# Another order of the parts of a pair of heads, and another start of the GLU, in an attention + soft-MoE + GLU kernel

## Chip, cores and metric

One Trainium2 chip, of which one core is used. The metric is the device time of one execution in microseconds; three executions of the kernel before took 492.02, 494.66 and 494.78 us, median 494.66 us.

## The reference

```python
# q, k, v: (4 batches, 8 heads, 576 tokens, 64)
q_rot, k_rot = rotate(q), rotate(k)                 # rope
attn = softmax(scale * q_rot @ k_rot.T) @ v         # -> x, 2304 tokens x 512
# soft MoE: 8 experts with 4 slots each, 512 -> 1024 -> 512
logits = x @ phi
d = softmax over the tokens (axis 0) of logits
slot_out[e] = maximum((d.T @ x)[e] @ w1[e], 0) @ w2[e]
y = (softmax over the slots of logits) @ slot_out
# "GLU": 512 -> 768 -> 512
h = maximum(maximum(y @ g1, y @ g2), y @ g3)
out = h @ w_out
```

## The kernel before, in words

All matmuls take float32 data; where full precision is wanted, a number is split into a high part (a cast to fp32r, on ACT) and a low part (the rest, on DVE or POOL), and the products of the parts are added up in PSUM.

**Attention.** The work goes by pairs of heads, 16 pairs `g`, each with nine units `n = 9*g + i`: a unit is 128 columns of scores (S, L342/L354 on PE), their maximum (L359 on DVE), the exponential (L371 on ACT), its transposition (T, L380/L382/L386 on PE) and the copy out of PSUM (Te, L403/L405 on ACT, L408/L411 on DVE). Then come the product with v (PV, L430/L433 on PE) into `u`, whose high part ACT takes (L442) and whose low part DVE takes (L440), a matmul that gives the tokens' x and their logits (L471), and sums for the softmax over all tokens of a batch.

The pair's inputs are made while the pair before it runs: POOL applies rope to q, k and the 64 rest tokens' rows r (L220 to L223), PE transposes them (L272 for q and k, L255 for r, tiles `tq<g>q`, `tq<g>k`, `tq<g>r`), ACT takes the high part (L283/L285), DVE the low part (L294/L297) into `qkt`, and SP's DMA queue stacks these into `qst` and `kst` (L303, eight transfers a pair), which the scores read.

**Weights.** Between these, 32 blocks of weights that come in an eight byte form are converted to float32 (tiles `raw`, `cv`, `cx`: ACT L596/L620, DVE L610, L613, L615, L618, POOL L622/L624, loads L582, stores L590 to `wod` and `wmd`). Two small DVE steps (L950, tile `xr`) make the low part of phi. SP also queues the loads of the expert weights (`wt`, L150), of q and k (L196), of their rest rows (`rr`, L186/L187) and of v (L202/L209). Each `wt` load takes the place of one whose last reader is done.

**What sets the order.** The program runs under a manual schedule: each part of each pair is put into one list with a time in units, `at_(9*g + value, part)`, the list is sorted, and that is the program order of every engine. The values are the table `TIMES`: for pairs 2 to 14 the same ones each, `first` for the opening (pairs 0 and 1), `last` for pair 15, `fill...` for the conversion, `loadw` for the weight loads. An engine takes its instructions in that order and waits on semaphores for what they need.

**Tail.** After the attention the slots' inputs go through the experts (h L742, its transposition L732, `ops` L758), limited by the weights' transfers; at the end of this stream SP queues the GLU's weights (L766/L768 `wm`, L771 `wof`). The MoE output is then multiplied with the GLU's first weights per slot (tiles `tq`, three PSUM banks, L801), so that a piece of 128 hidden columns costs one matmul of 128 rows for each of the three weights. `stacked(f)` splits such a piece: a cast on ACT (L814) and a subtraction on DVE (L815), into the tile of f: `ts8`, `ts9`, `ts23`, `tsxr`, `tslg`, `tssit` for f = 0 to 5; f and f+3 share a bank of `tq`. `prepare(f)` splits w_out's rows of piece f: a cast on ACT (L709), a subtraction on POOL (L710). `emit_h(k, f)` is three matmuls (L837, `g`), the maximum of three on DVE (L846; a copy on ACT and two DVE maxima, L842 to L844, for a few), then a split: cast on ACT (L856), subtraction on POOL (L857). Three matmuls for each 128 tokens and piece add to the output (L892, `r`). k = 0 is the 256 rest tokens, k = 1 to 4 are 512 tokens of a batch each. The `g` tiles are in two pools of three PSUM banks with one tile each; the first has banks that are free early, the second those of `tq`:

```python
i = run["h"] = run.get("h", -1) + 1
ps = ps_g[(i - 1) % 2 if i else 0].tile([128, 3, 512], F32, tag="g", name=f"g{k}_{f}")
```

## Time and profile before

| what | value |
|---|---|
| median of three executions | 494.66 us (492.02 to 494.78) |
| the profiled execution | 491.53 us |
| its span, first to last instruction | 489.70 us |
| outside the span | 1.83 us |
| PE busy | 466.1 us (95%) |
| DVE, ACT, POOL busy | 347.9, 293.7, 279.3 us |
| bytes moved | 105.67 MB, mean 216 GB/s |
| mean granted TensorE clock | 0.997 |

All rows below and all durations are of the one profiled execution; "idle before" is the time for which an engine stood before an instruction, and the arrow names what ended it. PE is the engine that is busy nearly always, with three stretches where it is not: the opening, the end of the weights' stream and the start of the GLU.

### The profile page before, as it was taken

The numbers are of one execution on the slowest core, as the hardware profiler recorded it, in microseconds if no ns is written. First come the engines' busy times: TensorE is split into PE (matmuls) and PEld (weight loads), VectorE is DVE, ScalarE is ACT, GpSimd is POOL, SyncE is SP. The second block draws the span as 40 slices with busy tenths as digits, with TensorE's granted clock in tenths as the row PEclk, the third lists the DMA queues.
The fourth block names the chain that finished last, engine by engine and source line by source line (L and its number), as shares of the span: only waits on it lengthen the run. The fifth ranks groups of instructions, "written<-read, shape, count | busy, mean of one in ns | idle before, by whom it ended". The sixth has DMA issues, their size and how long they took to land. (4 is left out here: it accounts for less than half of the span.)

```text
span 489.7 us, 9779 instructions
## 1 busy us (share of the span) xinstructions
PE 466.1 (95%) x3392; PEld 348.9 (71%) x3392; DVE 347.9 (71%) x663; ACT 293.7 (60%) x652; POOL 279.3 (57%) x374
## 2 busy tenths in 40 slices
PE   8789899999999999999999999998998799999996
PEld 7678677787786877868768777774334567888885
DVE  7869899987889889899989898566221367544520
ACT  2677688786887877788878778651201344322311
POOL 5989678878697796769986743011000276423420
PEclk9999999999999999999999999999999899999999
DMA  8589999998899899998987837999999401111111
GB/s 212 148 232 249 291 254 267 272 272 230 246 248 296 222 286 272 228 263 219 232 197 179 210 100 183 306 363 391 388 386 407 189 0 44 65 44 65 43 66 64
DMA packets 73121, 105.67 MB, mean 216 GB/s; under 512 B 12144, under 2 KB 41456, under 8 KB 72560
## 3 DMA queue, kind: packets, MB, share of 16 engines
q1 hardware_dynamic: 73072, 105.04, 74.5%
q8 instruction: 27, 0.44, 0.4%
q14 instruction: 22, 0.18, 0.1%
HBM read 66.98 MB, written 11.01 MB: 159 GB/s over the span
## 5 line engine op out<-in xcount | busy, mean ns | idle before, releaser
L359 DVE TENSOR_REDUCE nm<-s 128x1 f32<-128x576 f32 x144 | 107.7, 749 | 20.4 <-PE s L354 17.0
L371 ACT ACTIVATE P<-s,nm 128x576 f32<-128x576 f32 x144 | 106.9, 744 | 23.2 <-DVE nm L359 22.0
L354 PE MATMUL s<-kst,qst 128*128 128x288 f32 x600 | 108.2, 311 | 4.2 <-DMA kst<-qkt 1.5
L380 PE MATMUL s<-ident,P 128*128 128x128 f32 x576 | 90.9, 281 | 2.5 <-ACT P L371 2.3
L354 PEld LDWEIGHTS s<-kst,qst 128*128 128x128 f32 x600 | 85.0, 190 | 9.1 <-PE s L354 2.6
L380 PEld LDWEIGHTS s<-ident,P 128*128 128x128 f32 x576 | 63.9, 140 | 26.3 <-ACT P L371 14.3
L892 PE MATMUL r<-wo,h 128*128 128x512 f32 x324 | 79.7, 396 | 0.6 <-ACT h L856 0.2
L430 PE MATMUL u<-pt,vn 128*64 128x256 f32 (+1 forms) x512 | 72.2, 414 | 0.0
L892 PEld LDWEIGHTS r<-wo,h 128*128 128x128 f32 x324 | 61.2, 190 | 15.2 <-POOL h L857 0.9
L857 POOL TENSOR_TENSOR h<-hf,h 128x512 fp32r<-128x512 f32 (+1 forms) x30 | 35.4, 1181 | 45.3 <-ACT h L856 45.2
L846 DVE TENSOR_REDUCE hf<-g 128x512 f32<-128x1536 f32 (+1 forms) x26 | 40.8, 1599 | 28.1 <-PE g L837 23.9
L403 ACT COPY pt<-s 128x512 f32<-128x512 f32 x64 | 37.5, 585 | 22.6 <-PE s L380 21.3
L405 ACT COPY pt<-s 128x640 f32<-128x640 f32 x64 | 44.5, 695 | 7.8 <-PE s L382 7.5
L430 PEld LDWEIGHTS u<-pt,vn 128*64 128x64 f32 x512 | 32.5, 136 | 22.1 <-issue 5.1
L856 ACT CAST h<-hf 128x512 fp32r<-128x512 f32 (+1 forms) x30 | 17.3, 578 | 50.7 <-DVE hf L846 45.3
L622 POOL TENSOR_TENSOR raw<-raw 128x384 f32<-128x384 f32 x32 | 26.5, 828 | 36.3 <-ACT raw L620 30.2
L624 POOL TENSOR_TENSOR cv<-cv,raw 128x384 f32<-128x384 f32 x32 | 33.0, 1030 | 2.5
L710 POOL TENSOR_TENSOR wo<-wof,wo 128x512 fp32r<-128x512 f32 x6 | 7.6, 1280 | 44.5 <-ACT wo L709 44.5
L615 DVE SCALAR_TENSOR_TENSOR cv<-raw,cv 128x384 uint32<-128x384 uint32 x32 | 29.2, 912 | 0.4
L371 ACT ACTIVATION_READ_ACCUMULATOR P<-s,nm 128x1 f32 x144 | 28.7, 199 | 0.0
L471 PE MATMUL x<-xr,ut 128*128 128x256 f32 x160 | 26.4, 294 | 0.0
L471 PEld LDWEIGHTS x<-xr,ut 128*128 128x128 f32 x160 | 21.4, 189 | 1.0 <-DVE ut L440 0.2
(363 smaller groups left out, 761.6 us busy)
## 6 DMA issues: line engine op xcount, KB each, us to landing
wt<-in_moe_w_dram SPq DMA_DIRECT2D x32, 1024.0 KB, 10.0
qst<-qkt SPq DMA_DIRECT2D x60, 288.0 KB, 6.3
raw<-in_moe_w_dram SPq DMA_DIRECT2D x24, 384.0 KB, 5.3
kst<-qkt SPq DMA_DIRECT2D x30, 160.0 KB, 5.2
wmd<-cv SPq DMA_DIRECT2D x24, 192.0 KB, 4.1
kst<-qkt SPq DMA_DIRECT2D x30, 144.0 KB, 5.0
vn<-in_v_dram SPq DMA_DIRECT2D x16, 256.0 KB, 6.7
wm<-wmd SPq DMA_DIRECT2D x4, 1024.0 KB, 14.5
```

The lines of the kernel that those rows point to most:

```text
L354: nc.tensor.matmul(s[:, h, 0:288], l, r[:, 288 * h:288 * h + 288], start=(i == 0), stop=(i == len(todo) - 1))
L359: nc.vector.tensor_reduce(out=nm[n], in_=st[n][:, :, 0:288], axis=AX.XY, op=ALU.max, negate=True)
L371: nc.scalar.activation(out=dst.rearrange("p (h c) -> p h c", h=2), in_=s[:, :, 0:288], func=AF.Exp, bias=nm.pop(n), accum_out=acc)
L380: nc.tensor.transpose(s[:, 0, 128 * c:128 * c + 128], p[:, c0 + 128 * c:c0 + 128 * c + 128], ident)
L403: copy(out=o[:, 0:4, w + q0:w + q0 + 128], in_=src[:, 0:4, :])
L405: copy(out=o[:, 0:5, q0:q0 + 128], in_=src[:, 0:5, :])
L430: nc.tensor.matmul(u[r, 0:q1 - q0], vn[g][:, x, 64 * c:64 * c + 64], o[:, c, c0 + q0:c0 + q1], start=(c == 0), stop=False)
L471: nc.tensor.matmul(ps[:, 256 * i:256 * i + 256], utf[:, S * z + 128 * t:S * z + 128 * t + 128], xr[:, 0:hp + 2:hp + 1, :], start=(z == 0), ...
L624: nc.gpsimd.tensor_tensor(out=t3, in0=t3, in1=hf, op=ALU.add)
L846: nc.vector.tensor_reduce(out=h, in_=ps[:, :, 0:n].rearrange("p m n -> p n m"), axis=AX.X, op=ALU.max)
L857: nc.gpsimd.tensor_tensor(out=lo, in0=h, in1=hi.bitcast(F32), op=ALU.subtract)
L892: nc.tensor.matmul(p, a[:, s_], w, start=(f == 0 and z == 0), stop=(f == NF - 1 and z == 2))
```

## The change

All values of `TIMES` but a few are other numbers, so that the program order of the engines is another one; and the start of the GLU is written in another order. The code, and two lines of the table:

```diff
- 'loadw': -3.321369,
+ 'loadw': 15.022565,
- 'stackk': -4.533007,
+ 'stackk': -6.992883,
...
-        for f in range(2):
-            prepare(f)
+
+        FO = [0, 1, 3, 4, 2, 5]
+        prepare(0)
...
-            if f == 0:
+            if k not in hid:
...
-            ps = ps_g[(i - 1) % 2 if i else 0].tile([128, 3, 512], F32, tag="g", name=f"g{k}_{f}")
+            ps = ps_g[(i - 1) % 2 if i > 2 else 0].tile([128, 3, 512], F32, tag="g", name=f"g{k}_{f}")
...
-        for f in (0, 1, 3, 4):
+        for f in (0, 1, 3):
             stacked(f)
-        emit_h(0, 0)
+        prepare(1)
+        emit_h(0, 0, (0,))
+        stacked(4)
+        emit_h(0, 0, (1,))
+        emit_h(0, 1, (0,))
         stacked(2)
+        emit_h(0, 1, (1,))
         stacked(5)
-        emit_h(0, 1)
...
-                for f in range(NF):
+                for z0, f in enumerate(range(NF) if k else FO):
                     while rows and rows[0][0] <= step:
-                        emit_h(*divmod(rows.pop(0)[1], NF))
-                    if k == 0 and f + 2 < NF:
-                        prepare(f + 2)
+                        k_, f_ = divmod(rows.pop(0)[1], NF)
+                        emit_h(k_, f_ if k_ else FO[f_])
+                    if k == 0 and z0 + 2 < NF:
+                        prepare(FO[z0 + 2])
...
-                            nc.tensor.matmul(p, a[:, s_], w, start=(f == 0 and z == 0), stop=(f == NF - 1 and z == 2))
+                            nc.tensor.matmul(p, a[:, s_], w, start=(z0 == 0 and z == 0), stop=(z0 == NF - 1 and z == 2))
```

`emit_h(k, f, (0,))` is the matmuls and the maximum alone, `(1,)` the split alone. The piece order of k = 0 is now 0, 1, 3, 4, 2, 5, and of the `g` tiles the first four (i = 0 to 3) are in the first pool and i = 4 is the first in the second pool, where before i = 2 was.

Set side by side, the two program orders differ in four stretches.

**The opening, pairs 0 to 2.** DVE before, from the second maximum of pair 0 (`nm1`) to the fifth (`nm4`); `cx0`, `cv0` and `raw0` are the conversion of the first block, `xr` is phi's low part:

```order
L359 TENSOR_REDUCE nm1_274<-s1_266 128x1
L610 TENSOR_SCALAR cx0_286<-cv0_284 128x3x128
L613 TENSOR_SCALAR cv0_284<-cx0_286 128x384
L294 SCALAR_TENSOR_TENSOR qkt_109<-tq1q_297,qkt_109 128x512
L359 TENSOR_REDUCE nm2_312<-s2_290 128x1
L950 TENSOR_TENSOR xr_65<-early_106,xr_65 64x4x32
L297 TENSOR_TENSOR qkt_109<-tq1r_323,qkt_109 128x2x2x64
L615 SCALAR_TENSOR_TENSOR cv0_284<-raw0_276,cv0_284 128x384
L359 TENSOR_REDUCE nm3_342<-s3_328 128x1
L950 TENSOR_TENSOR xr_65<-early_106,xr_65 64x4x32
L297 TENSOR_TENSOR qkt_109<-tq1k_351,qkt_109 128x512
L618 TENSOR_SCALAR raw0_276<-cv0_284 128x3x128
L359 TENSOR_REDUCE nm4_393<-s4_366 128x1
```

DVE now, the same stretch (L956 is L950 of before):

```order
L359 TENSOR_REDUCE nm1_274<-s1_266 128x1
L294 SCALAR_TENSOR_TENSOR qkt_109<-tq1q_292,qkt_109 128x512
L359 TENSOR_REDUCE nm2_300<-s2_285 128x1
L297 TENSOR_TENSOR qkt_109<-tq1r_317,qkt_109 128x2x2x64
L359 TENSOR_REDUCE nm3_331<-s3_323 128x1
L956 TENSOR_TENSOR xr_65<-early_106,xr_65 64x4x32
L610 TENSOR_SCALAR cx0_343<-cv0_341 128x3x128
L613 TENSOR_SCALAR cv0_341<-cx0_343 128x384
L615 SCALAR_TENSOR_TENSOR cv0_341<-raw0_276,cv0_341 128x384
L956 TENSOR_TENSOR xr_65<-early_106,xr_65 64x4x32
L618 TENSOR_SCALAR raw0_276<-cv0_341 128x3x128
L359 TENSOR_REDUCE nm4_384<-s4_333 128x1
```

The six instructions that stood one by one between the maxima now stand in a row between the fourth and the fifth. On ACT the first block's cast (L596) that stood between the first two exponentials comes after the third.

SP's queue before, from the stacking of pair 2's q on:

```order
L303 DMA qst0_101<-qkt_109 64x2x576 x4
L186 DMA rr1_649<-in_q_dram 64x8x64
L187 DMA rr1_649<-in_k_dram 64x8x64
L590 DMA wod_71<-cv2_503 128x384
L582 DMA raw5_681<-in_moe2_w_out_dram 128x256
L582 DMA raw5_681<-in_moe2_w_out_dram 128x2x256
L303 DMA kst0_103<-qkt_109 64x576 x2
L303 DMA kst0_103<-qkt_109 64x640 x2
L196 DMA qn4_716<-in_q_dram 128x2x256
L196 DMA kn4_718<-in_k_dram 128x2x256
L150 DMA wt1_730<-in_moe_w1_dram 128x4x512
```

and now:

```order
L303 DMA qst0_101<-qkt_109 64x2x576 x4
L303 DMA kst0_103<-qkt_109 64x576 x2
L303 DMA kst0_103<-qkt_109 64x640 x2
L590 DMA wod_71<-cv2_500 128x384
L582 DMA raw5_675<-in_moe2_w_out_dram 128x256
L582 DMA raw5_675<-in_moe2_w_out_dram 128x2x256
L196 DMA qn4_679<-in_q_dram 128x2x256
L196 DMA kn4_681<-in_k_dram 128x2x256
L186 DMA rr1_688<-in_q_dram 64x8x64
L187 DMA rr1_688<-in_k_dram 64x8x64
```

The four transfers of `kst` for pair 2 come right behind those of `qst`, ahead of two loads of rest rows, a store and two or three loads; the first `wt` load of this place is gone: the first ten such loads stand two pairs later than before, and so does the rest of the row until the end of the attention, where the last 22 stand as before.

**Pairs 2 to 15.** One thing moves: the rest rows' transposition, cast and subtraction (`tq<g>r`) go from behind the last products of the pair before to right behind the first scores of the new pair, and POOL's rope takes r after k. ACT before, at the start of pair 8 (`s72` is its first unit, `s70` and `u7` belong to pair 7):

```order
L620 ACTIVATE raw17_2115<-raw17_2115 128x3x128
L596 ACTIVATE cv18_2393<-raw18_2220 128x384
L405 COPY pt1_7_2322<-s70_2346 128x5x128
L371 ACTIVATE P0_110,sums8_2420<-s72_2406,nm72_2412 128x576
L442 CAST ut_112<-u7_0_2382 128x256
L285 CAST qkt_109<-tq9r_2430 128x2x2x64
L403 COPY pt0_8_2450<-s72_2406 128x4x128
L371 ACTIVATE P0_110,sums8_2420<-s73_2434,nm73_2448 128x576
```

and now:

```order
L596 ACTIVATE cv18_2397<-raw18_2216 128x384
L405 COPY pt1_7_2322<-s70_2346 128x5x128
L285 CAST qkt_109<-tq9r_2412 128x2x2x64
L371 ACTIVATE P0_110,sums8_2426<-s72_2407,nm72_2421 128x576
L442 CAST ut_112<-u7_0_2372 128x256
L403 COPY pt0_8_2450<-s72_2407 128x4x128
L371 ACTIVATE P0_110,sums8_2426<-s73_2431,nm73_2448 128x576
```

The cast of `tq9r` (L285) stands ahead of the first exponential of the pair, no longer behind `ut`. On DVE the subtraction of r (L297) stands likewise ahead of that of `ut` (L440).

**Pair 15** has its last sums and x parts in a slightly other order; SP's last stores and loads and the 22 `wt` loads are as before.

**The GLU's start.** ACT before (`h40_0` and `h6_0` are the high parts of k = 0, `hf0_f` the maxima of its piece f, `wo422` and `wo6` those of w_out):

```order
L709 CAST wo422_5016<-wof0_4883 128x512 x2
L814 CAST ts8_5023<-tq0_4924 64x384
L814 CAST ts9_5024<-tq1_4925 64x384
L814 CAST tsxr_5026<-tq0_4924 64x384
L814 CAST tslg_5027<-tq1_4925 64x384
L856 CAST h40_0_5050<-hf0_0_5057 128x256
L814 CAST ts23_5025<-tq2_4926 64x384
L814 CAST tssit_5028<-tq2_4926 64x384
L856 CAST h40_0_5050<-hf0_1_5069 128x256
L709 CAST wo422_5016<-wof0_4883 128x512
L856 CAST h40_0_5050<-hf0_2_5087 128x256
L709 CAST wo422_5016<-wof0_4883 128x512
```

and now (L815 and L857 are L814 and L856 of before):

```order
L709 CAST wo422_5016<-wof0_4883 128x512
L815 CAST ts8_5021<-tq0_4924 64x384
L815 CAST ts9_5022<-tq1_4925 64x384
L815 CAST tsxr_5024<-tq0_4924 64x384
L709 CAST wo422_5016<-wof0_4883 128x512
L815 CAST tslg_5025<-tq1_4925 64x384
L857 CAST h40_0_5048<-hf0_0_5055 128x256
L815 CAST ts23_5023<-tq2_4926 64x384
L857 CAST h40_0_5048<-hf0_1_5065 128x256
L815 CAST tssit_5026<-tq2_4926 64x384
L709 CAST wo422_5016<-wof0_4883 128x512
L857 CAST h40_0_5048<-hf0_3_5087 128x256
```

One cast of w_out stands ahead of the first piece's cast instead of two, the second after three pieces. DVE before:

```order
L815 TENSOR_TENSOR ts8_5023<-tq0_4924,ts8_5023 64x384
L815 TENSOR_TENSOR ts9_5024<-tq1_4925,ts9_5024 64x384
L815 TENSOR_TENSOR tsxr_5026<-tq0_4924,tsxr_5026 64x384
L815 TENSOR_TENSOR tslg_5027<-tq1_4925,tslg_5027 64x384
L846 TENSOR_REDUCE hf0_0_5057<-g0_0_5053 128x256
L815 TENSOR_TENSOR ts23_5025<-tq2_4926,ts23_5025 64x384
L815 TENSOR_TENSOR tssit_5028<-tq2_4926,tssit_5028 64x384
L846 TENSOR_REDUCE hf0_1_5069<-g0_1_5065 128x256
L846 TENSOR_REDUCE hf0_2_5087<-g0_2_5083 128x256
L846 TENSOR_REDUCE hf0_3_5103<-g0_3_5099 128x256
L846 TENSOR_REDUCE hf0_4_5111<-g0_4_5107 128x256
```

and now (L816 and L847 are L815 and L846 of before):

```order
L816 TENSOR_TENSOR ts8_5021<-tq0_4924,ts8_5021 64x384
L816 TENSOR_TENSOR ts9_5022<-tq1_4925,ts9_5022 64x384
L816 TENSOR_TENSOR tsxr_5024<-tq0_4924,tsxr_5024 64x384
L847 TENSOR_REDUCE hf0_0_5055<-g0_0_5051 128x256
L816 TENSOR_TENSOR tslg_5025<-tq1_4925,tslg_5025 64x384
L847 TENSOR_REDUCE hf0_1_5065<-g0_1_5061 128x256
L816 TENSOR_TENSOR ts23_5023<-tq2_4926,ts23_5023 64x384
L816 TENSOR_TENSOR tssit_5026<-tq2_4926,tssit_5026 64x384
L847 TENSOR_REDUCE hf0_3_5087<-g0_3_5083 128x256
L847 TENSOR_REDUCE hf0_4_5103<-g0_4_5099 128x256
L847 TENSOR_REDUCE hf0_2_5111<-g0_2_5107 128x256
```

The first maximum stands behind three subtractions (before: four), the second behind four (before: six), and the piece of `tsxr` is the third to be reduced, that of `ts23` the fifth.

## Rows read from the trace of the kernel before

**Rows 1.** Busy time of each engine by stretch, with granted clock, DMA share, GB/s.
```profile
core 0: us, PE busy (x) PEld busy (x) DVE busy (x) ACT busy (x) POOL busy (x), PEclk, DMA share, GB/s
...
56.00:306.00 250.00, 246.76 (x1956) 190.75 (x1954) 223.84 (x463) 200.44 (x458) 188.25 (x259) 1.00 0.90 236
...
340.00:386.00 46.00, 43.04 (x396) 18.21 (x396) 10.11 (x22) 9.13 (x16) 1.53 (x3) 1.00 1.03 387
...
414.00:489.70 75.70, 71.84 (x316) 58.93 (x314) 28.00 (x20) 20.21 (x35) 22.56 (x18) 1.00 0.15 56
```
**Rows 2.** Timeline, end of the weights' stream: start, us, engine line op, [idle before <-releaser].
```profile
371.72 1.06 PE L758 MATMUL ops<-wt,hts 128*32 128x512 f32 x8 [1.66 <-DMA wt<-in_moe_w_dram]
383.85 1.25 ACT L709 CAST wo<-wof 128x512 fp32r<-128x512 f32 x2 [2.48 <-DMA wof<-wod]
```
**Rows 3.** Timeline, the opening (pair 0), on DVE and PE.
```profile
15.68 0.55 DVE L610 TENSOR_SCALAR cx<-cv 128x384 f32<-128x384 f32 x1 [0.68 <-ACT cv L596]
...
18.27 0.98 DVE L950 TENSOR_TENSOR xr<-early,xr 64x128 fp32r<-64x128 f32 x1
...
19.62 1.23 DVE L615 SCALAR_TENSOR_TENSOR cv<-raw,cv 128x384 uint32<-128x384 uint32 x1
...
20.78 0.74 DVE L359 TENSOR_REDUCE nm<-s 128x1 f32<-128x576 f32 x1
...
23.97 1.41 DVE L359 TENSOR_REDUCE nm<-s 128x1 f32<-128x576 f32 x2
...
36.81 0.76 PE L354 MATMUL s<-kst,qst 128*128 128x288 f32 x4 [0.38 <-DVE pt L411]
```
**Rows 4.** One line, L615, all its 32 instructions: min/median/max in ns.
```profile
L615 DVE SCALAR_TENSOR_TENSOR cv<-raw,cv x32: 539/770/1678, 19.6 to 296.4; 128x384 uint32<-128x384 uint32 x32
```
**Rows 5.** Timeline, stacking of pair 2: SP's queue, DVE's low part, PE's first scores.
```profile
46.81 3.45 SPq L303 DMA_DIRECT2D kst<-qkt  x4
...
42.70 0.68 DVE L297 TENSOR_TENSOR qkt<-tq2k,qkt 128x512 fp32r<-128x512 f32 x1
...
54.30 0.77 PE L354 MATMUL s<-kst,qst 128*128 128x288 f32 x4 [1.47 <-DMA kst<-qkt]
```
**Rows 6.** Timeline, ACT at the start of two pairs.
```profile
172.15 0.74 ACT L371 ACTIVATE P<-s,nm 128x576 f32<-128x576 f32 x1 [0.45 <-DVE nm L359]
...
173.14 0.38 ACT L285 CAST qkt<-tq9r 128x256 fp32r<-128x256 f32 x1
...
212.53 0.73 ACT L371 ACTIVATE P<-s,nm 128x576 f32<-128x576 f32 x1
```
**Rows 7.** Timeline, the GLU's start.
```profile
385.01 0.84 ACT L814 CAST ts<-tq 64x384 fp32r<-64x384 f32 x2
386.12 0.62 PE L837 MATMUL g<-cst,ts 128*128 128x256 f32 x3 [0.80 <-DVE ts L815]
...
387.14 0.55 DVE L815 TENSOR_TENSOR tslg<-tq,tslg 64x384 fp32r<-64x384 f32 x1
387.72 0.96 DVE L846 TENSOR_REDUCE hf<-g 128x256 f32<-128x768 f32 x1
...
388.82 0.98 PE L837 MATMUL g<-cst,ts 128*128 128x256 f32 x3 [2.09 <-DVE hf L846]
...
389.60 2.62 PE L892 MATMUL r<-wo,h 128*128 128x512 f32 x6
...
391.38 0.96 DVE L846 TENSOR_REDUCE hf<-g 128x256 f32<-128x768 f32 x1
...
395.24 1.82 DVE L846 TENSOR_REDUCE hf<-g 128x256 f32<-128x768 f32 x2 [1.66 <-PE g L837]
...
400.43 5.09 DVE L846 TENSOR_REDUCE hf<-g 128x512 f32<-128x1536 f32 x3 [1.62 <-PE g L837]
```
**Rows 8.** Stretch of 4 us in the GLU's start, as in rows 1.
```profile
388.00:392.00 4.00, 3.17 (x9) 2.72 (x10) 2.41 (x4) 1.35 (x3) 0.73 (x1) 0.57 0.00 0
```
**Rows 9.** Chain that ended last, its last piece on PE: start, us, what.
```profile
468.84 17.01 PE r L892 x75
```

More of the change, by code (lines that the diff above doesn't have):

```diff
@@ L15 @@
 PSUM = bass.MemoryType.PSUM
-TIMES = {'PV0': [6.553131, 6.989132, 7.498326, 7.544825, 8.190408],
[4 rows of a table removed]
- 'den': 9.357116,
- 'dveT': [8],
- 'end': [15.707371, 16.548506, 17.994015, 18.892372],
- 'exp': [-0.944455, -1.054367, -1.085271, -0.586941, -0.745122, -0.797759, -0.979385, -0.489266, -1.259442],
- 'fill': [-1.203776, 0.690077, 0.880261, 0.962634, 1.922644, 4.229447, 4.947705, 5.639369, 6.514506, 7.419095],
- 'fill0': [-34.440716, -0.550009, 2.059553, 5.488154, -33.812723, 5.00556, 6.374143],
- 'fillb': [0.775254, 1.659994, 1.945723, 4.894894, 7.188337],
[3 rows of a table removed]
-           'exp': [-2.562309, -35.382874, -3.774496, -2.438842, -1.194014, -2.065725, -1.75621, -0.776184, -0.948378],
-           'lok': -7.989044,
-           'loq': -13.52447,
-           'lor': -10.13142,
-           'max': [-1.645758, -1.835256, -4.857215, -3.058265, -1.686503, -2.550164, -2.563383, -1.829256, -1.460128],
-           'qkk': -8.323103,
-           'qkq': -38.764171,
-           'qkr': -10.799686,
-           'stackk': -5.135993,
-           'stackq': -9.866356},
+TIMES = {'PV0': [6.052698, 6.539022, 6.831161, 7.041179, 8.370574],
[4 rows of a table added]
+ 'den': 9.045966,
+ 'dveT': [8],
+ 'end': [15.996553, 16.470809, 18.107722, 18.802385],
+ 'exp': [-0.675131, -0.916498, -1.127766, -0.304154, -0.913015, -1.011578, -0.953932, -0.243716, -1.040539],
+ 'fill': [-1.316643, 0.146837, 0.779834, 0.899125, 1.252142, 4.242488, 5.036954, 5.844713, 6.810021, 7.369609],
+ 'fill0': [-2.965317, 1.274402, 1.506862, 5.137451, -0.677174, 3.405875, 5.934943],
+ 'fillb': [0.263554, 0.659419, 1.262914, 4.782657, 7.03104],
[3 rows of a table added]
+           'exp': [-7.893717, -27.924269, -6.082201, -4.622187, -0.966764, -1.860446, -1.972664, 0.213131, -0.679221],
+           'lok': -6.168845,
+           'loq': -22.133635,
+           'lor': -13.346412,
+           'max': [-1.919995, 40.189116, -13.728982, -6.819962, -1.88512, -1.867328, -2.393284, -1.184347, -1.911995],
+           'qkk': -8.826648,
+           'qkq': -23.658995,
+           'qkr': -13.35598,
+           'stackk': -5.63826,
+           'stackq': -11.947606},
  'h': [0, 0, 0.5, 1.5, 2, 2, 3.5, 4, 5.5, 5.0, 6.0, 6.5, 9.0, 10, 12.5, 18, 18.5, 24.0, 32.5, 40, 39, 44.5, 45, 51, 57, 58, 60.0, 68.0,
@@ L46 @@
  'hact': [[2, 2], [2, 5], [2, 1], [0, 5]],
- 'last': {'PV1': [12.664366, 12.934353, 17.22414, 26.110192, 26.547594],
-          'PV1b': [8.769912, 9.062373, 9.151216, 14.754356, 15.203461],
-          'den': [8.56153, 7.905642],
-          'end': [21.775382, 31.063865, 43.298229, 64.732682],
-          'endb': [54.132671, 67.122919, 68.341622, 68.342622],
-          'lg': [11.933538, 44.986281],
-          'u1': [28.197427, 28.198635],
-          'u1b': [19.012823, 27.127678],
-          'warm': [[35.239871, 4], [53.731771, 4], [53.840437, 4]],
-          'x': [9.796981, 33.594561, 32.137697],
-          'xe': [[11.762713, 13.454033], [34.190229, 67.803844], [32.726764, 67.108962]]},
@@ L77 @@
- 'u1': [10.949512, 11.364858],
+ 'last': {'PV1': [13.362323, 23.757612, 27.866613, 32.577903, 34.487854],
+          'PV1b': [9.034314, 9.623589, 9.670028, 10.656968, 11.314749],
+          'den': [12.059624, 7.065112],
+          'end': [15.553272, 40.986824, 53.411692, 75.731423],
+          'endb': [111.764265, 112.019026, 114.008368, 119.095903],
+          'lg': [14.02684, 62.06959],
+          'u1': [35.240849, 35.241849],
+          'u1b': [29.443596, 31.049719],
+          'warm': [[57.500286, 4], [57.655604, 4], [97.595993, 4]],
+          'x': [11.566386, 42.509109, 34.56566],
+          'xe': [[12.445342, 30.186802], [51.307524, 53.750567], [57.173325, 55.473275]]},
@@ new lines @@
+ 'lg': [15.366289],
+ 'loadqk': -22.678765,
+ 'loadr': -22.34179,
+ 'loadv': -1.873124,
+ 'loadw': 15.022565,
+ 'lok': -7.015135,
+ 'loq': -11.030046,
+ 'lor': -9.491336,
+ 'max': [-1.11053, -1.080468, -1.701921, -1.209456, -0.992138, -1.336195, -0.990138, -0.989138, -1.184604],
+ 'onact': [1, 0, 0],
+ 'qkk': -8.083624,
+ 'qkq': -12.675556,
+ 'qkr': -10.180993,
+ 'ropek': -16.364586,
+ 'ropeq': -17.904547,
+ 'roper': -14.747196,
+ 'stackk': -6.992883,
+ 'stackq': -8.503989,
+ 'u0': [8.703314, 8.807017],
@@ L78 @@
+ 'u1': [10.743395, 11.315174],
  'warm': [0, 0],
```

22 lines of the change are left out of this document (3 added, 19 removed), and 14 rows, old and new, of the table TIMES.

## The prediction

> **What bounds the kernel now.** I read the busy times by stretch first. From 56 to 306 us, the steady part of the attention, PE works 246.76 of 250 us, which is 98.7%, with DVE at 90% and ACT at 80%; from 414 us to the end it works 71.84 of 75.70 us [rows 1]. In both a PE that is kept supplied is the bound. From 340 to 386 us the DMA engines are full, at a share of 1.03 and 387 GB/s [rows 1], and the timeline of the end of that stretch shows PE waiting 1.66 us for a weight transfer and ACT 2.48 us for w_out's first rows [rows 2]: there the stream of weights is the bound. So whatever makes the attention end earlier starts this stream earlier, and the tail with it; whatever only frees PE within the stream is worth nothing.
>
> What can be gained lies where PE is not supplied. I looked for it in the timelines of three places: the opening, where PE's last wait of pair 0 is 0.38 us for a DVE copy [rows 3]; the first scores of pair 2, which wait 1.47 us for the transfer of `kst` [rows 5]; and the GLU's start, where PE's three matmuls of the first piece begin at 386.12, those of the second at 388.82 and the second maximum only at 391.38 [rows 7]. After it the chain that ended last is PE alone: its last piece is 75 output matmuls in 17.01 us, 0.227 us each [rows 9]. An earlier start of the GLU is therefore carried to the end.
>
> **The opening.** Six DVE instructions move from between the maxima into one row ahead of the fifth: three passes of 0.55, one of 1.23, and two of 0.98 for phi (I price the second as the first) [rows 3], together 4.84 us. Before, the fourth maximum ended at 20.78 + 0.74 = 21.52 and the fifth began at 23.97. If the fourth stays where it was, the fifth begins at 21.52 + 4.84 = 26.36, 2.4 later. If it moves up by all that stood ahead of it (0.55 + 0.55 + 0.98 + 1.23 = 3.31), the fifth begins at 23.05, 0.9 earlier. The fourth maximum's row shows no idle time ahead of it, so DVE's own queue held it and it will move up, but its scores and the matmuls ahead of them on PE allow only a part. I take 0, between the ends and nearer to the lower; bounds -0.9 and +2.4. What absorbs a small delay is the first scores' wait of 0.38 us for DVE at 36.81.
>
> Why the ends are far apart: the longest of the conversion's DVE passes, L615, took from 539 to 1678 ns, median 770, for one and the same shape [rows 4]. The Trainium skill, "SBUF — State Buffer", section "Who interferes with whom", says that a DVE instruction with two inputs in SBUF contends with a GpSimd instruction that reads SBUF. The spread agrees with it, L615 has two inputs and POOL ropes beside it; by that rule the row of six would meet POOL's rope with three of its members, and the 1.23 could be 1.68, which would put the fifth maximum 0.45 later and the total at 490.6.
>
> **The stacking of pair 2.** SP's queue is in order. Before, `kst` stood behind two loads of rest rows, a store and conversion loads and was issued from 46.81, for 3.45 us, while its data, the low part on DVE, was ready at 42.70 + 0.68 = 43.38 [rows 5]. Now it stands right behind `qst`, so it can be issued at about 43.4, 3.4 us earlier. The scores waited 1.47 us, so the wait goes as a whole, and 1.9 us are left over. What is late next is PE's own work ahead of it. What was passed (rest rows, a store, conversion loads) comes 3.5 us later and is needed in the next pair or later. I take -1.4; bounds -1.47 and 0.
>
> **Pairs 2 to 15.** The cast of the rest rows (0.38 us) now stands ahead of the pair's first exponential. At 172.15 this exponential waited 0.45 us for its maximum, so the cast fits; at 212.53 it followed without a gap, so there it costs 0.38 [rows 6]. Fourteen pairs at 0.38 are 5.3 us as the upper end. The lower end is 0, since PE's work is the same and PE is the bound. I take 0, because PE has products of the pair before and the second unit's scores to run while the exponential is late. POOL makes r after k instead of before, a few us later, while its transposition was not waited for; also 0. The weight loads that come two pairs later use a queue and DMA engines that are not full (share 0.90 in that stretch [rows 1]) and are read only in the tail: 0. Pair 15's other order lies ahead of the stream, ±0.5.
>
> **The GLU's start.** First maximum: two casts of w_out took 1.25 us ahead of the pieces' casts [rows 2]; one stays, so all moves up by 0.62, and the maximum stands behind three subtractions instead of four, another 0.55 [rows 7]: 387.72 - 0.62 - 0.55 = 386.55. Second maximum: it needs the bank of the first, which is read until 386.55 + 0.96 = 387.51; before, the matmuls began 388.82 - (387.72 + 0.96) = 0.14 after this; with the 0.62 that the first piece's took, the second maximum can begin at about 388.3, against 391.38, where two more subtractions and their casts lay ahead: -3.1. Behind it, the same four maxima and the first of k = 1 follow, plus those two subtractions (1.1 us). Before, DVE idled 1.66 us ahead of 395.24 and 1.62 us ahead of 400.43 [rows 7], in which they fit. The third and fourth `g` have to take the one early bank set in turn, each for one maximum, so DVE and PE alternate there; before, the third could use the other set, but only once `tq` was read. So k = 1 begins to be reduced at about 397.3 instead of 400.43. From 414 us PE is the bound, so this is kept. I take -3.1; bounds -1.2 (only the first maximum's gain) and -3.7 (a walk in which the casts of the later pieces move up too).
>
> **Sum.** 489.70 - 1.4 - 3.1 = 485.2 us of span, with the 1.83 us around it 487.0, which is 4.5 less than the profiled execution's 491.53. That execution lies 3.1 below the median of 494.66, so the forecast in the median's terms is 494.66 - 4.5 = 490.2 us. About 1% (4.9 us) is what a measurement of this kernel can tell from no change.
>
> **Rivals.**
> *The clock falls again.* From 388 to 392 us the granted clock was 0.57, close to the lower level of 1.2 GHz, after PE had done little from 385 on [rows 8], and six output matmuls took 2.62 us [rows 7] where the full pace is 6 x 0.227 = 1.36. The new start has the same lull before it, shorter by some 1.2 us. If the clock falls, the second piece's matmuls take 0.98 instead of 0.62, and the six output matmuls, which stand ahead of the third piece on PE, 1.26 more: -3.1 + 1.6 = -1.5, in all -2.9, 491.8 us. For it: the row. Against it: PE gets work back from about 387.6 on. The Trainium skill, "TensorE: Matmul & The Clock Gate", section "What's actually happening", says that the default state is throttled and activity releases the throttle; the row agrees that the clock fell behind a lull, and by that rule alone a short lull would do the same again.
> *The stacking brings nothing*, because the opening loses about as much (its upper end is above the 1.47) or because another wait stands in its place: -3.1, 491.6 us.
> *Only the first maximum comes earlier*, since the second is held by its one bank set and by casts on ACT in their new order: -1.2 - 1.4 = -2.6, 492.1 us.
> *Slower: the rest rows' cast and subtraction stand ahead of the chain at the turn of each pair.* On ACT 0.38 ahead of the exponential, on DVE as much ahead of the low part of `ut`, for which PE's x matmuls wait: 0.76 x 14 = 10.6, less 4.5, is +6.1, 500.8 us. It decides where ACT's idle time ahead of the exponential is under 0.38 in most of the pairs and PE finds nothing else in its order. For it: the row at 212.53. Against it: the row at 172.15, and PE has had other work at such places, as 98.7% busy shows.
>
> **How the numbers follow.** Chances: the forecast 0.42, the clock 0.24, the stacking 0.16, only the first maximum 0.08, slower 0.10. The likeliest case's own range is 488.0 to 491.8, from the bounds of its terms. The range of 487.6 to 494.5 takes in the first four cases with an opening that costs up to its upper end, and leaves out most of the slower one and the small chance that the clock stays full and the opening gains. Faster by over 1% (below 489.7) is nearly half of the forecast's own case and little of the next two, 0.30; slower by over 1% (above 499.6) is most of the slower case, 0.07; the rest, 0.63, lies within 1%.
>
> **What would show it.** Right: the first scores of pair 2 without a DMA wait, and the fifth maximum of pair 0 near 24; the same length of a pair in steady state; w_out's first cast about 1.4 earlier; from there 3.1 less to the first maximum of k = 1, and a clock of 1.00 in the GLU's start. Wrong: idle time of PE for the exponential at the turn of pairs, longer pairs, a wait for another transfer at pair 1 or 2, a first w_out cast that is no earlier, or a clock near 0.5 again.

## The result, and the profile after

| | executions | median, us | lowest to highest |
|---|---|---|---|
| before | 4 | 494.48 | 492.02 to 494.78 |
| changed | 4 | 487.63 | 486.27 to 490.64 |

The ratio is 0.987, 95% interval 0.983 to 0.992: 1.3% faster, 6.9 us between the medians. The forecast was 490.2 us, 4.5 us less than before, with a range of 487.6 to 494.5. The sign is right, and the median lies inside the range by 0.03 us only; it is 0.4 below the forecast's own case (488.0 to 491.8), and "faster by over 1%" had a chance of 0.30. The size is half as large again as forecast, and it does not come from where the sum put it. Every ratio in this document is of executions in the faster of two states that a few kernels showed, while the medians take in all executions.

The profiled execution of the changed kernel took 488.54 us, its span 486.80, 2.9 us under the span before. It is one of the slower executions of its kernel, while the profiled one of before (491.53) is faster than any of the four above; so the two traces show less than the medians do. Its stretches, to be set beside [rows 1], with granted clock, DMA share and GB/s at the end of each line:

```profile
core 0: us, PE busy (x) PEld busy (x) DVE busy (x) ACT busy (x) POOL busy (x), PEclk, DMA share, GB/s
...
34.00:56.00 22.00, 21.91 (x165) 16.67 (x167) 20.06 (x45) 17.19 (x40) 18.84 (x27) 1.00 0.77 200
56.00:306.00 250.00, 246.07 (x1945) 190.03 (x1942) 220.40 (x455) 200.03 (x456) 188.33 (x257) 1.00 0.90 241
...
340.00:386.00 46.00, 44.23 (x395) 18.75 (x387) 10.24 (x19) 9.50 (x17) 1.28 (x1) 0.97 1.00 377
...
414.00:486.80 72.80, 68.86 (x303) 56.48 (x301) 26.78 (x18) 18.62 (x32) 20.86 (x17) 0.99 0.15 58
```

PE bounds the attention and the end as before, the weights' stream the part between. The first of these rows had no counterpart among those shown of before; it is this one:

```profile
34.00:56.00 22.00, 20.15 (x155) 15.60 (x153) 18.92 (x38) 16.50 (x39) 17.04 (x25) 1.00 1.07 257
```

What moved is seen by following a few marks through both traces: the first maximum of a pair, w_out's first cast, the first maximum of k = 1.

| start of | before | changed | difference |
|---|---|---|---|
| pair 1, first maximum | 34.45 | 33.22 | -1.2 |
| pair 2 | 55.11 | 52.14 | -3.0 |
| pair 3 | 74.16 | 71.13 | -3.0 |
| pair 4 | 92.67 | 91.71 | -1.0 |
| pair 15 | 308.40 | 307.15 | -1.3 |
| w_out's first cast | 383.85 | 383.33 | -0.5 |
| GLU, first maximum | 387.72 | 386.10 | -1.6 |
| GLU, first maximum of k = 1 | 400.43 | 397.42 | -3.0 |

So 3.0 us are gained up to pair 2, 2 lost again in pair 3, 0.7 between pair 15 and w_out's first cast, and 2.5 gained at the GLU's start. The timeline of the changed kernel in the opening and up to pair 2, which answers to [rows 3] and [rows 5]:

```profile
19.23 0.27 DVE L956 TENSOR_TENSOR xr<-early,xr 64x128 fp32r<-64x128 f32 x1
...
21.01 0.74 DVE L615 SCALAR_TENSOR_TENSOR cv<-raw,cv 128x384 uint32<-128x384 uint32 x1
21.78 0.71 DVE L956 TENSOR_TENSOR xr<-early,xr 64x128 fp32r<-64x128 f32 x1
...
22.99 0.75 DVE L359 TENSOR_REDUCE nm<-s 128x1 f32<-128x576 f32 x1
...
21.29 1.05 POOL L221 TENSOR_TENSOR rot<-qn,rp 128x256 f32<-128x256 f32 x1
...
40.55 3.96 SPq L303 DMA_DIRECT2D kst<-qkt  x4
...
51.07 0.76 PE L354 MATMUL s<-kst,qst 128*128 128x288 f32 x4
```

The row of six on DVE costs 3.8 us from 19.23 to 22.99, not the 4.84 that I summed, as the two-input instructions took 0.27, 0.74 and 0.71 instead of the 0.98, 1.23 and 0.98 of my sum. The fifth maximum begins at 22.99, 1.0 earlier. Beside L615 and the L956 behind it, a POOL instruction of the rope (L221) takes 1.05 us, where the one of this place took 0.73 in the trace before. The Trainium skill, "SBUF — State Buffer", "Who interferes with whom", says that a DVE instruction with two inputs in SBUF contends with a GpSimd instruction that reads SBUF. These rows agree with it; here it was POOL that paid, which the lateness of 0.45 that I worked out from that rule left out. In the trace before both had paid: beside the L615 of 1.23 us the rope's L220 took 1.04 us, and 0.74 in the changed kernel. `kst` is issued from 40.55, and the first scores of pair 2 start without a wait.

The loss in pair 3 is a chain that the trace of before did not show. Timeline of the changed kernel:

```profile
73.77 0.34 SPq L590 DMA_DIRECT2D wod<-cv  x1
...
80.84 0.55 ACT L596 ACTIVATE cv<-raw 128x384 f32<-128x384 f32 x1 [1.53 <-POOL raw L622]
...
82.24 0.80 PE L354 MATMUL s<-kst,qst 128*128 128x288 f32 x4 [1.27 <-ACT pt L403]
```

and that store among its DMA issues, with KB and us from issue to landing:

```profile
wod<-cv SPq DMA_DIRECT2D x1, 192.0 KB, 7.0
```

The store of a converted block, issued at 73.77, lands 7.0 us later, at 80.77. Ahead of it in the queue stands a load of 1 MB (`wt`), issued at 68.98, which lands at 78.82. The cast L596 writes a new block into that one of the two buffers `cv` which this store still reads; it stands at the head of ACT's queue from 79.31, and starts at 80.84, 0.07 us after the landing. (The row names POOL's L622, which had ended 0.6 earlier.) The copy behind it on ACT comes late, and PE waits 1.27 us for that.

In the stream the granted clock is the other thing. The timeline and the window of the first expert matmuls:

```profile
339.01 3.46 PE L742 MATMUL h<-wt,sitxr 128*32 128x512 f32 x16 [0.38 <-DVE sitxr L648]
```

```profile
340.00:344.00 4.00, 4.00 (x28) 1.04 (x24) 3.06 (x6) 0.74 (x1) 0.00 (x0) 0.67 1.05 387
```

In the trace before, the 16 took 1.92 us at full clock:

```profile
339.95 1.92 PE L742 MATMUL h<-wt,sitxr 128*32 128x512 f32 x16 [0.38 <-DVE sitxr L648]
```

Here they took 3.46, with a clock of 0.67 over these 4 us. The transfers absorb most of that, as they are the bound there: from this instruction to w_out's first cast it is 0.4 us more than before.

The GLU's start, to be set beside [rows 7] and [rows 8]:

```profile
383.33 0.62 ACT L709 CAST wo<-wof 128x512 fp32r<-128x512 f32 x1 [2.47 <-DMA wof<-wod]
...
386.10 0.96 DVE L847 TENSOR_REDUCE hf<-g 128x256 f32<-128x768 f32 x1
...
387.63 1.93 PE L898 MATMUL r<-wo,h 128*128 128x512 f32 x6
387.83 0.96 DVE L847 TENSOR_REDUCE hf<-g 128x256 f32<-128x768 f32 x1 [0.19 <-PE g L838]
...
397.42 5.09 DVE L847 TENSOR_REDUCE hf<-g 128x512 f32<-128x1536 f32 x3 [1.62 <-PE g L838]
```

```profile
388.00:392.00 4.00, 3.65 (x18) 2.53 (x17) 2.86 (x4) 1.95 (x5) 2.33 (x3) 1.00 0.00 0
```

Counted from w_out's first cast, the first maximum begins at 2.77 (before 3.87), the second at 4.50 (7.53), the first of k = 1 at 14.09 (16.58); the clock stays at 1.00.

### The profile page after: what moved, and what is told of

Same layout as the page of the kernel before. It is cut to its first block, busy times and chain, and to the rows that moved or that the text cites. A ratio compares the mean times of both kernels' runs of the same rounds, so it can differ in the third digit from the quotient of the medians.

```text
span 486.8 us, 9778 instructions
## 1 busy us (share of the span) xinstructions
PE 466.3 (96%) x3392; PEld 347.8 (71%) x3392; DVE 345.4 (71%) x663; ACT 294.4 (60%) x652; POOL 282.6 (58%) x374
## 4 chain that ended last, share of the span: by engine, by line
PE 62%; DMA 13%; DVE 9%; ACT 8%; issue 3%; POOL 3%; SPq 2%; ACTq 0%; DVEq 0%; POOLq 0%
PE r L898 14%; PE s L354 11%; PE u L430 10%; PE s L380 9%; DMA qst<-qkt 3%; PE h L742 3%; DMA wof<-wod 3%; PE g L838 3%; ACT P L371 3%; PE u L433 2%; DMA kst<-qkt 2%; PE x L471 2%; DVE hf L847 2%; DMA wmd<-cv 2%; SPq L768 1%
## 5 line engine op out<-in xcount | busy, mean ns | idle before, releaser
L898 PE MATMUL r<-wo,h 128*128 128x512 f32 x324 | 78.6, 391 | 0.4 <-ACT ob L862 0.2
L847 DVE TENSOR_REDUCE hf<-g 128x512 f32<-128x1536 f32 (+1 forms) x26 | 40.9, 1600 | 27.0 <-PE g L838 22.8
L405 ACT COPY pt<-s 128x640 f32<-128x640 f32 x64 | 44.6, 697 | 8.0 <-PE s L382 7.6
L622 POOL TENSOR_TENSOR raw<-raw 128x384 f32<-128x384 f32 x32 | 27.1, 848 | 37.2 <-ACT raw L620 31.3
L857 ACT CAST h<-hf 128x512 fp32r<-128x512 f32 (+1 forms) x30 | 17.3, 578 | 48.2 <-DVE hf L847 42.8
L615 DVE SCALAR_TENSOR_TENSOR cv<-raw,cv 128x384 uint32<-128x384 uint32 x32 | 27.5, 859 | 0.4
L610 DVE TENSOR_SCALAR cx<-cv 128x384 f32<-128x384 f32 x32 | 17.5, 547 | 7.8 <-ACT cv L596 7.6
```

Of the source, the lines that this page charges most:

```text
L405: copy(out=o[:, 0:5, q0:q0 + 128], in_=src[:, 0:5, :])
L847: nc.vector.tensor_reduce(out=h, in_=ps[:, :, 0:n].rearrange("p m n -> p n m"), axis=AX.X, op=ALU.max)
L898: nc.tensor.matmul(p, a[:, s_], w, start=(z0 == 0 and z == 0), stop=(z0 == NF - 1 and z == 2))
```

## The experiments

Twelve runs were made, in three groups, each beside the kernel before on the same chip (medians there 494.94, 494.20 and 494.35 us). In most of them the table of times is printed over more lines, so that their line numbers are 28 higher.

**The changed kernel again.** No edit.

> The changed kernel once more, with a second profile, to tell what of its trace repeats. Theory A (places fixed by the order): pair 1 begins its maxima near 33.2 us, pair 2 near 52.1, then pair 3 loses about 2 us again (pair 4 near 91.7) because the store of a converted block lands 7 us after its issue; w_out's first cast comes only 0.5 us earlier than before; the GLU's start gains 2.5 us. Time 487 to 488.5 us. Theory B (chance: clock and transfers differ from execution to execution): the half clock at 339 to 342 us is absent or in another place, w_out's first cast moves by up to 1 us, and pair 3's loss is absent; time between 485 and 490 us.

Measured: 487.26 us, ratio 0.985 (0.981 to 0.988). Pair 1 begins at 33.29 and pair 2 at 52.23, as in the first trace, but pair 3 takes 19.0 us instead of 20.6, and pair 15 begins at 305.50, 2.9 earlier than before. w_out's first cast is at 381.70, 2.2 earlier, and k = 1 at 395.74, 4.7 earlier. So the opening's gain and the GLU's repeat, and pair 3's loss does not: the same store, issued at 73.84 behind the same load of 1 MB, lands at 78.2.

```profile
wod<-cv SPq DMA_DIRECT2D x1, 192.0 KB, 4.4
```

The load itself took 7.7 us to land here and 9.8 in the first trace; why is open, but the program order does not decide it. Each theory holds for one part: A for the opening and the GLU, B for pair 3. Two of B's signs did not come: the first expert matmuls took 3.46 us again, and w_out's first cast moved by 1.6 us.

**The table alone.** The new `TIMES` in the old code.

```diff
- TIMES = { ... of the kernel before }
+ TIMES = { ... of the changed kernel }
```

> The new table of times with the old start of the GLU. Theory A (two gains that add up): the attention's part gains what the changed kernel shows until w_out's first cast, 0.5 to 1.5 us, and the GLU's start is as before, so about -1 us against the kernel before, 493.5 us. Theory B (the opening's 3 us are kept except for chance): -2 to -3 us, 492 us. Theory C (the table gains nothing to the end, as the weights' stream hides it): 0.

Measured: 489.83 us, ratio 0.990 (0.986 to 0.994), 5.1 us less than before: all theories put the gain too low. Pair 2 at 52.07, no pair with a late transfer, w_out's first cast at 381.05; the GLU's start as of old (k = 1 17.0 behind that cast).

**The GLU's start alone.** The old `TIMES` in the new code.

> The old table with the new start of the GLU. Theory A: the first maximum of k = 1 comes 3.0 us after w_out's first cast earlier than before less nothing, that is 14.1 us behind that cast where before it was 16.6 (a gain of 2.5), and the time falls by 2.5 to 3.7 us, to 491 to 492 us. Theory B (the gain of the changed kernel there is only that the clock stayed full, as before lost 1.3 us to half clock): the gain is 1.2 us, about 493.3 us.

Measured: 492.55 us, ratio 0.996 (0.993 to 0.999), 2.4 us less. From the first cast to k = 1 it is 14.04 us, as in the changed kernel, which is theory A's number; how much of it is the clock, theory B's cause, is weighed in the part on the prediction. The two parts add up: 5.1 + 2.4 = 7.5, and both together took off 7.7. Its profile also shows what the old table does in other executions than the profiled one: pair 7 takes 21.6 us where it took 19.05, by the same chain as above (PE waits 1.94 us behind this cast).

```profile
167.18 0.55 ACT L624 ACTIVATE cv<-raw 128x384 f32<-128x384 f32 x1 [1.65 <-DMA wmd<-cv]
```

```profile
wmd<-cv SPq DMA_DIRECT2D x1, 192.0 KB, 6.8
```

**The opening alone.** Only `first`, `xr` and `fill0` of the new table in the kernel before.

> Only the opening of the new table (values of pairs 0 and 1, phi's parts, the conversion's first block) in the kernel before; the stacking of pair 2 and the weight loads as before. Theory A (my forecast: opening 0): pair 1 begins at 34.4 us and pair 2 at 55.1. Theory B (the changed trace): pair 1 begins its maxima at 33.2, 1.2 us earlier; pair 2's scores still wait for kst, 1.5 us or more, since this wait takes up what the opening gives, so pair 2 near 54 to 55. Time within 1% of the kernel before.

Measured: 496.06 us, ratio 1.002 (0.999 to 1.005). Pair 1 begins at 33.53, 0.9 earlier, so theory B has that; but pair 2 at 57.40, 2.3 later than before, which neither had. PE's wait and the landing times of `kst`:

```profile
56.06 1.30 PE L382 MATMUL s<-kst,qst 128*128 128x288 f32 x4 [2.95 <-DMA kst<-qkt]
```

```profile
kst<-qkt SPq DMA_DIRECT2D x2, 160.0 KB, 6.2
kst<-qkt SPq DMA_DIRECT2D x2, 144.0 KB, 7.4
```

The same transfers had taken 5.8 and 6.6 us before, and the wait of 1.47 became 2.95. That is 1.5 of the 3.2 us by which pair 1 is longer. Another 1.07 is a wait of PE in pair 1 for ACT, whose cast waited 1.46 us until a store had landed:

```profile
44.13 0.79 PE L382 MATMUL s<-kst,qst 128*128 128x288 f32 x4 [1.07 <-ACT pt L431]
```

Most of the rest is in the scores themselves, which took 1.30 us at a granted clock of 0.50 instead of 0.77. So an earlier opening made nothing earlier here. It is one profile, and of the slowest of ten executions.

**The weight loads' place alone.**

```diff
- 'loadw': -3.321369,
+ 'loadw': 15.022565,
```

> The kernel before with one number changed: the ten early weight loads stand two pairs later. Theory A (transfers are served in the order of issue, so a load of 1 MB put ahead of a pair's stacking makes it land later; without the two early ones pair 2's kst lands in time even though it stands behind the rest rows): pair 2's wait for kst, 1.47 us before, is gone or under 0.4, pair 2 begins at 53.6 to 54.0, and the time is 1 to 3 us under the kernel before, 492 to 494 us. Theory B (the order of the stacking decides, not the load): pair 2 still waits 1 us or more and begins at 54.8 to 55.2; time as before.

Measured: 494.76 us, ratio 1.001 (0.998 to 1.005). In the trace `kst` lands 5 us after its issue, and pair 2 begins at 54.07 without a wait for `kst`, 1.0 earlier than before: theory A is right on the wait. But pair 11 takes 20.87 us (before 18.96) with ACT's cast waiting 1.45 for a store, and in the time nothing is left.

```profile
kst<-qkt SPq DMA_DIRECT2D x2, 160.0 KB, 5.0
kst<-qkt SPq DMA_DIRECT2D x2, 144.0 KB, 4.9
```

**The stacking's order alone.**

```diff
- 'stackk': -4.533007,
+ 'stackk': -6.75,
```

> The kernel before with one number changed: the stacking of k goes right behind that of q (pair 2, and four other places where it passed rest rows or a store). The weight loads stay early. Theory B (my forecast): pair 2's wait of 1.47 us goes, pair 2 begins near 53.6, time -1.4 us, 493.5 us. Theory A (the early load of 1 MB delays the landing): the transfers are issued from 44 us and land 7 to 8 us later, at 52 to 53, so that a wait of 0 to 0.5 us is left; time -1 to -1.5 us. The two differ by less than the noise of a time here; what tells them apart is the landing time of kst and the wait in front of pair 2.

Measured: 494.04 us, ratio 1.002 (0.999 to 1.005). Pair 2's wait is gone and it begins at 54.34, 0.8 earlier; with the early load of 1 MB the transfers take this long:

```profile
kst<-qkt SPq DMA_DIRECT2D x2, 160.0 KB, 5.6
...
kst<-qkt SPq DMA_DIRECT2D x2, 144.0 KB, 6.2
```

The gain is lost in pair 3 (19.9 us instead of 18.5, ACT's cast waits 1.19). Either edit ends the wait that I priced at 1.4, and neither makes the kernel faster.

**The early weight loads back in the changed kernel.**

```diff
- 'loadw': 15.022565,
+ 'loadw': -3.321369,
```

> The changed kernel with the weight loads early again, as before; all else new. Theory A: with the 1 MB loads at 33 and 52 us back, kst of pair 2 lands at about 51 to 53 instead of 46 to 48, pair 2 begins 0 to 1.5 us later than 52.1, and more of the later pairs lose 1 to 2.5 us to a store or a stacking that lands late: time 1 to 4 us above the changed kernel, 488.5 to 491.5 us. Theory B (the loads' place is worth nothing): within 0.5 us of the changed kernel, pair 2 at 52.1.

Measured: 494.57 us, ratio to before 1.001 (0.998 to 1.004): 7.3 us slower than the changed kernel, more than theory A gave. Pair 2 begins at 52.49, 0.3 later, so its stacking is not the place. Pairs 2, 3 and 10 lose 2.5, 0.9 and 2.1 us against the second trace of the changed kernel. The first of these, behind the load that is issued at 51 us:

```profile
60.55 0.55 ACT L624 ACTIVATE cv<-raw 128x384 f32<-128x384 f32 x1 [3.17 <-DMA wod<-cv]
...
61.87 0.66 PE L408 MATMUL s<-ident,P 128*128 128x128 f32 x4 [1.67 <-ACT P L399]
```

So the loads, which I had priced at 0, are needed: with them early, more than the table's gain is lost (the GLU's new start alone, with the old table, took 492.55 on another chip). They do not suffice, as the run of the weight loads' place alone shows: late loads in the old table are worth nothing that can be measured. What else of the table they need was not tried.

**The rest rows back.** First with rope, transposition and ACT's cast moved back, DVE's subtraction left ahead.

```diff
- 'qkr': -10.180993, 'lor': -9.491336, 'ropek': -16.364586, 'ropeq': -17.904547, 'roper': -14.747196,
+ 'qkr': -9.443095, 'lor': -9.341195, 'ropek': -15.527989, 'ropeq': -17.598403, 'roper': -16.954151,
```

> The changed kernel with the rest rows' transposition and cast back behind the pair's first exponential, and POOL's rope on r ahead of k again. Theory A (my forecast, worth 0): pairs 2 to 15 take the same time within 0.5 us where no transfer is late, time within 1 us of the changed kernel (487.3 us). Theory B (the rival: each pair pays for the cast ahead of its exponential): up to 5 us faster than the changed kernel. Theory C (the new place is a gain): up to 3 us slower.

Measured: 509.98 us, ratio 1.033 (1.028 to 1.039). None of the theories: it is 22.7 us slower than the changed kernel. DVE stands for the cast that now comes late, and in ten pairs PE waits 0.91 us for what stands behind it on DVE. The one of pair 2:

```profile
56.33 0.42 DVE L325 TENSOR_TENSOR qkt<-tq3r,qkt 128x256 fp32r<-128x256 f32 x1 [1.47 <-ACT qkt L313]
...
57.23 1.83 PE L458 MATMUL u<-pt,vn 128*64 128x320 f32 x12 [0.91 <-DVE ut L468]
```

Then with DVE's part moved as well (`'qkr': -9.61`, `'lor': -9.15`):

> The changed kernel with all four parts of the rest rows' move undone together: POOL's rope on r ahead of k, PE's transposition behind the last products of the pair before, ACT's cast behind the first exponential, and (not in the run before) DVE's subtraction behind that of ut. Theory A (my forecast: worth 0; the 22 us of the run before came from DVE's subtraction left ahead in its queue, so that DVE stood there for a cast which now came late): median within 1.5 us of the changed kernel's 487.3, pairs without a late transfer as long as in the changed kernel within 0.2 us. Theory C (the new place of the rest rows itself is worth several us): 490 us or more, with waits in most pairs.

Measured: 497.65 us, ratio 1.007 (1.003 to 1.011), 10.4 us slower than the changed kernel. Pairs 1 to 4 are at most 0.2 us longer than there (18.96, 19.15, 18.46, 19.04 against 18.94, 18.99, 19.01, 19.14), as theory A has it, but the time is theory C's, and pairs 5, 6, 8 and 12 lose 1.6 to 2.9 us each. The queue of SP and POOL's rope in pair 5 show how it starts:

```profile
121.25 0.53 SPq L224 DMA_DIRECT2D qn<-in_q_dram  x1
126.30 0.37 SPq L224 DMA_DIRECT2D kn<-in_k_dram  x1
...
121.71 0.46 POOL L251 TENSOR_TENSOR rot<-rot,rr 128x128 f32<-128x128 f32 x1
...
125.00 1.28 POOL L251 TENSOR_TENSOR rot<-rot,kn 128x512 f32<-128x512 f32 x1
```

and the same place in the second trace of the changed kernel:

```profile
121.65 1.10 SPq L196 DMA_DIRECT2D kn<-in_k_dram  x1
...
120.20 1.28 POOL L223 TENSOR_TENSOR rot<-rot,kn 128x512 f32<-128x512 f32 x1
```

The load of the next k waits until POOL has roped the last: 125.00 + 1.28 = 126.28, issued at 126.30. Everything behind it in SP's queue (rest rows, a store, a load of 1 MB, the next stacking) comes about 3 us later, and the next stores meet the cast late. This run does not settle how much of the 10.4 us is r's place: with the old values for all three ropes, the rope on the q of pairs 7, 9 and 14 too went behind a conversion block on POOL. The first of these is made in pair 5, and begins late:

```profile
116.06 0.73 POOL L248 TENSOR_TENSOR rot<-qn,rp 128x256 f32<-128x256 f32 x1
```

There k's rope ends 4.8 us later than in the changed kernel, of which r ahead of it is 1.6 (120.48 to 122.12); the other two are made in pairs 7 and 12, at or next to the other pairs that lose. So q's place may be the larger part; that is not shown.

**The old bank rule.** In the changed kernel:

```diff
- ps = ps_g[(i - 1) % 2 if i > 2 else 0].tile(
+ ps = ps_g[(i - 1) % 2 if i else 0].tile(
```

> The changed kernel with the old rule for the banks of the g tiles: the third piece's matmuls take the second pool, whose banks hold tq until the last piece is split. Theory A (the alternation of four pieces on one set of banks is what lost 0.6 us of the 3.1 that I forecast there): the first maximum of k = 1 comes 13.4 to 13.7 us behind w_out's first cast instead of 14.05. Theory B (the new rule is needed, as the third piece would wait for the last split): 14.4 to 15 us. Theory C: 14.05, no difference. The time differs by at most 1 us from the changed kernel's 487.3.

Measured: 487.40 us, ratio 0.988 (0.983 to 0.992), the changed kernel's time. In its profile k = 1 comes 15.22 us behind the first cast, a little above theory B's 14.4 to 15, but not for its reason: the clock had fallen to half ahead of the third piece.

```profile
385.32 2.80 PE L926 MATMUL r<-wo,h 128*128 128x512 f32 x6
388.27 1.00 PE L866 MATMUL g<-cst,tsxr 128*128 128x256 f32 x3
```

```profile
387.02:389.02 2.00, 1.85 (x6) 1.08 (x5) 0.60 (x2) 1.09 (x2) 1.38 (x2) 0.50 0.00 0
```

The third piece's matmuls start without idle time behind the six of the output. So the bank rule can't be read from this trace; in the time it is worth nothing that can be measured.

**The conversion's cast later.** In the changed kernel and in the one before, the cast stands one step later, and DVE's first two passes stand together.

```diff
+            if i:
+                store(i - 1)
+                absolute(i)
+                yield
             t0 = t0s.pop(i)
...
-            if i:
-                store(i - 1)
...
-            absolute(i + 1)
```

> The changed kernel, with the first cast of each converted block one step later in the program (with the store that it follows, ahead of DVE's first two passes, which now stand together). Theory A (pairs that lose about 2 us are those in which this cast stands at the head of ACT's queue until the store two blocks back has landed): ACT's waits of over 0.5 us at this cast are gone or fewer and shorter, no pair shows a PE wait over 0.7 us, median 485.5 to 487.3 us, not slower than the changed kernel. Theory B (the lost time comes from somewhere else, or the later cast makes DVE wait as long): 487.3 us or slower.

> The same edit in the kernel before. Theory A: as the kernel before loses more to such waits (its profiled execution, 491.5 us, had none, its median is 494.5), the median falls by 1 to 3 us, to 491.5 to 493.5 us. Theory B: no change, 494.5 us.

Measured: 489.94 us, ratio to before 0.993 (0.990 to 0.996), 2.7 slower than the changed kernel; and 497.87 us, ratio 1.008 (1.004 to 1.012). In the changed kernel ACT's waits of over 0.5 us at this cast are gone, as theory A says, but DVE now stands for it, and three times PE waits over 1 us for DVE (theory B). In the kernel before, with the same edit, one wait of 2.13 us at this cast is left. The first of the three:

```profile
52.38 0.55 DVE L640 TENSOR_SCALAR cx<-cv 128x384 f32<-128x384 f32 x1 [0.85 <-ACT cv L624]
```

```profile
55.35 0.77 PE L382 MATMUL s<-kst,qst 128*128 128x288 f32 x4 [1.23 <-DVE pt L439]
```

That the store's landing holds ACT is thus shown in the rows; that the kernel gets faster by taking this wait away is not, as this edit put another in its place. A third buffer for these blocks was not tried. No version that ran beats the changed kernel.

## Why the prediction was right, and where it was not

- **The opening, taken as 0.** It was -0.9 to -1.3 us at pair 1 in the kernels with the new opening and the rest of the new table (33.14 to 33.57), and -0.9 with the old rest. The block on DVE cost 3.8 instead of 4.84 us; the second L950, which I priced as the first, had taken 0.83. The fifth maximum's -1.0 lay just outside my lower bound of -0.9.
- **The stacking of pair 2, -1.4.** The wait went, as forecast. But the first trace has the opening's 1.2 and this wait added up (-3.0 at pair 2), where I had let the two stand side by side. The opening alone shows that they depend on each other: without earlier transfers the wait was twice as long.
- **The weight loads two pairs later, priced at 0.** This is the step that failed. I argued that queue and DMA engines were not full at a share of 0.90. That is a mean over 250 us; around 34 to 56 us, where the first two loads stood (issued at 33.1 and 51.7), the share was 1.07, and it is 0.77 there in the changed kernel. Put back into the changed kernel they cost 7.3 us. Moved alone in the old table they gave nothing, and neither did the opening or the stacking alone: I added up terms as if they were independent, but the table's 5.1 us come only from several of them together, and which is not known.
- **Pairs 2 to 15, taken as 0 because PE is the bound.** Right for a pair in which every transfer is in time: without a late one each pair takes the same time in both orders within 0.8 us, nine of thirteen within 0.2 (before against the second trace of the changed kernel). What I missed is that executions of the kernel before can contain pairs that lose about 2 us to a late store (pair 7 in the run with the old table and the new GLU start), and the profiled execution had none. The table took 5.1 us off the median: 3.0 stand in the opening in the four profiles with the new order and late loads, the other 2 I put down to fewer late pairs, which is not shown. The traces agree with it (of four profiles with the new order and late loads only the first shows such a pair), but four profiles do not measure a frequency. More moved in these pairs than "One thing moves" says: SP's queue changed too, as at 122 us, where the loads of q and k (128.8 before, 122.5 now) passed those of the rest rows (121.9 and 124.7).
- **The slower rival, the rest rows' cast ahead of the exponential.** It did not come. A run with DVE and ACT out of step shows the kind of loss, 22.7 us; in the changed kernel cast, subtraction and transposition move together. Undone as a whole the move cost 10.4 us, q's rope included, so no loss by it shows here.
- **The GLU's start, -3.1.** It is -2.5 between w_out's first cast and k = 1, in five of the six profiles of the new start at full clock (14.04 to 14.09 against 16.56 to 17.02 in six of the old; the sixth, 15.18, has the cast earlier against the products in `tq`), and 2.4 in the time. These 2.5 are not the order's alone, as all six old starts ran with a fall of the clock: the two new starts with one took 14.8 and 15.2, which is 1.4 to 1.7 less than the old 16.6; the other 0.8 to 1.2 come only where the clock stays full. The gain is kept to the end: from k = 1 to the last output matmul it is 85.4 us in every trace. First and second maximum came as worked out (-1.1 and -3.0 for -1.17 and -3.1); what I did not price is that behind the second the new order takes 9.6 us to k = 1, the old one 9.05.
- **The rival of the clock.** In six of six profiles with the old start the clock was at about half within 4 to 10 us behind w_out's first cast; with the new start it was full in six of eight profiles and half in two. So neither the forecast's case nor the rival's is the only one. The Trainium skill ("TensorE: Matmul & The Clock Gate", "What's actually happening") says that the throttled state is the default and that activity releases it. The falls agree with it, as they came behind the lull at the GLU's start (PE was busy 27% of the time from 385 to 388.5 in the trace before), but with the new start like lulls ended both ways: from 1.3 to 4.7 us behind w_out's first cast PE was busy 48% of the time in the run of the old bank rule, where the clock then fell, and 47% in the changed kernel with the later cast, where it stayed full. Where it fell with the new start, k = 1 came 14.8 and 15.2 us behind the cast, 0.8 to 1.2 later; I had said 1.6.
- **The sum** went from profile to profile, 4.5 us, and was then set on the median. The profiled execution of before lay 3 us below its median, which I carried over as a constant; the changed kernel's lay 0.9 above its own. The two profiled executions differ by 3.0, and the other 3.9 of the gain of 6.9 are these two offsets; that the change removed part of what makes the old kernel's executions differ would explain it, and is not shown (the changed kernel's six in the second run still spread from 486.67 to 490.39, the 23 of before beside them from 491.34 to 497.84). By parts the table gave 5.1 where the sum had 1.4, and the GLU's start 2.4 where it had 3.1. That the median falls into the range is in part luck.

## What to carry to other kernels

Read the DMA share in the stretch where a queue's loads stand, not its mean (1.07 against 0.90 here). Loads of 1 MB that nobody needed soon stood in front of stores and stackings, and an engine that reused a buffer waited for such a store, with everything behind it in its queue. Terms that share a queue are not independent: here three edits gave nothing alone, and taking one of them back cost more than the whole table gave. Where the profiled execution is faster than the median, look for what it was spared, as a change may act on just that. Move all parts of a chain (transposition, cast, subtraction) together: with one left ahead in its engine's queue the kernel took 22.7 us more, with all moved back 10.4.
